# Two last blocks of a retention and MLP kernel: a third first-layer group as seven products, the second layer started inside the first, and own banks for its third product

## The chip, the cores and the metric

One core of a Trainium2 chip runs the whole program. The metric is the device time of one execution in microseconds (us): the median of three runs of the kernel before is 298.36 us (298.1 to 300.1).

## The reference

Eight batches of eight heads, 576 positions, head width 64, go through a causal retention (scores times a decay mask, no softmax). Its output, regrouped to 4608 tokens of 512 features, goes through a two-layer MLP with a tanh gelu between the layers:

```python
scores = scale * q @ k.T                       # per batch and head
ret = scores * Dmat                            # Dmat[i, j] = gamma_h ** (i - j) for i >= j, else 0
x = (ret @ v).transpose(0, 2, 1, 3).reshape(4608, 512)
h = x @ w_in                                   # 512 -> 2048
g = 0.5 * h * (1 + tanh(c * (h + 0.044715 * h**3)))
out = g @ w_out                                # 2048 -> 512
```

## The kernel before

The tokens are worked off in nine blocks of 512 (`NTB` = 9; the code calls a block `t`). Blocks 0 to 7 hold the first 512 positions of the eight batches; block 8 holds the last 64 positions of all of them, the tails. While the MLP of one block runs, the attention of the next batches is threaded in between: `at(t, u, f)` books a piece of work for step `u` of block `t`, and the loop at the end of the kernel runs it when that step has been issued. Nothing reorders the work after that: each engine executes its instructions in the order in which the code issues them, so the order in the loop is the order on TensorE (PE), VectorE (DVE), ScalarE (ACT) and on the store queues of SP and ACT.

**First layer.** `up(t, fc)` computes one group of 128 of the 2048 hidden features for all 512 tokens: four matmuls 128x512 into one PSUM bank `hp` (L471), then one gelu on ACT (L477) into `gT`. In blocks 7 and 8 (`WIN`) the first two double groups are instead done by `up_prod(t, j, m)`: the 2x2 block product over tokens x features is made by seven products instead of eight (a Strassen-Winograd scheme). One product is four matmuls 128x256 (L560). The seven products of group `j` go into three banks hA, hB and hC; between them ACT copies a bank to SBUF (L580, L586), DVE adds (L567) or copies (L588), and four gelus (L570) write `gT`. The operand sums of the weights (`in_sums`, L517) and of the tokens (`x_sums`, L536) are made on DVE beforehand, in the second layer of block 6 and of the block before. `W_ORDER` is the order by hand: "12" is product 2 of group 1, an empty token is one `up`, "a2" is `act_sums` for group 2.

**Second layer.** It is done by seven products too, in all blocks from 1 on. `act_sums` (L643 to L646) makes four sums of `gT` per group of two features on DVE, the third of them in place. `prod(t, m, u)` is product `m` for token half `u`: eight matmuls 128x256 (L661), with banks opA to opD. `after(t, m, u)` empties them: after product 1 an ACT copy (L691) keeps bank A, product 2 then goes on adding into the same bank, and a second ACT copy (L707) writes the lower half of output tile `o0`; DVE adds (L675) make the rest. In blocks 7 and 8 the order of products is 1, 4, 6, 5, 7, 2, 3, each for both halves. Products 5 and 3 share bank C: 3 adds on top of 5.

**Stores.** A block's two output tiles leave by `send`. For block 8 `send` calls `end` (L688), which writes 64 rows of one batch per DMA, one on SP's queue and one on ACT's: four DMAs of 128 KB for `o1` after product 7, four of 64 KB for the lower half of `o0` after product 2, and two plus two of 64 KB after the two halves of product 3.

PSUM has eight banks; `bank` takes the one longest free, `drop` gives it back at once in issue order, and the next user waits on the chip for the last reader.

Of the kernel before, what the change touches and what calls it, by code (L numbers as in the profile page):

```python
# [20 lines left out]
def kernel(  # L21
# [476 lines left out]
        )  # L498
        drop(hp)

    WIN = {t: 2 for t in (NTB - 2, NTB - 1)}
    GW = max(WIN.values())
    wi = {}

    def in_sums(j, ns):
        if not wi:
            for n in "234":
                wi[n] = sb.tile([128, 2, 256 * GW], F16, tag="ld", name="wi" + n, bufs=LD)
        c, lo, hi = slice(256 * j, 256 * j + 256), slice(256 * j, 256 * j + 256), slice(DF // 2 + 256 * j, DF // 2 + 256 * j + 256)
        b11, b12, b21, b22 = w_in_sb[:, 0:2, lo], w_in_sb[:, 0:2, hi], w_in_sb[:, 2:4, lo], w_in_sb[:, 2:4, hi]  # L510
        t2, t3, t4 = (wi[n][:, :, c] for n in "234")
        for n in ns:
            o, x, y, f = {
                3: (t3, b22, b12, ALU.subtract), 2: (t2, t3, b11, ALU.add),
                4: (t4, b21, t2, ALU.subtract), 1: (b12, b12, b11, ALU.subtract),
            }[n]
            nc.vector.tensor_tensor(out=o, in0=x, in1=y, op=f)  # L517
# [3 lines left out]
    def x_sums(t):  # L521
        if not xw:
            for n in ("12", "34"):
                x = sb.tile([128, 2, 4, 2, TL], F16, tag="ld", name="x" + n, bufs=LD)
                xw[int(n[0])], xw[int(n[1])] = x[:, 0], x[:, 1]
            for n in range(2):
                for s in "svu":
                    wk[s, n] = sb.tile([128, 512], F32, tag="ld", name="w" + s, bufs=LD)
        o = 8 * (t % 2) if t < B else GM
        x = xT[:, o : o + 8]  # L530
        a11, a12, a21, a22 = x[:, 0:4, 0:2], x[:, 0:4, 2:4], x[:, 4:8, 0:2], x[:, 4:8, 2:4]
        for s, x, y, f in (
            (xw[1], a21, a22, ALU.add), (xw[2], xw[1], a11, ALU.subtract),
            (xw[3], a11, a21, ALU.subtract), (xw[4], a12, xw[2], ALU.subtract),
        ):
            nc.vector.tensor_tensor(out=s, in0=x, in1=y, op=f)  # L536

    wk, wb = {}, {}

    def up_prod(t, j, m):  # L540
        if t not in gT:
            gT[t] = sb.tile([128, NF, NI, 128], F16, tag="gT", name="gT", bufs=1)
        o = 8 * (t % 2) if t < B else GM
        lo, hi = 256 * j, DF // 2 + 256 * j
        xh = lambda u, k: lambda kt: xT[:, o + 4 * u : o + 4 * u + 4, 2 * k + kt, :]
        xs = lambda n: lambda kt: xw[n][:, :, kt, :]
        ws = lambda k, c: lambda kt, i: w_in_sb[:, 2 * k + kt, c + 128 * i : c + 128 * i + 128]
        wt_ = lambda n: lambda kt, i: wi[n][:, kt, lo + 128 * i : lo + 128 * i + 128]
        tag, x, w = {
            1: ("B", xh(0, 0), ws(0, lo)), 2: ("A", xh(0, 1), ws(1, lo)), 3: ("C", xs(4), ws(1, hi)),  # L550
            4: ("B", xh(1, 1), wt_("4")), 5: ("C", xs(1), ws(0, hi)), 6: ("B", xs(2), wt_("2")),
            7: ("B", xs(3), wt_("3")),
        }[m]
        new = m in (1, 2, 5)
        if new:
            wb[j, tag] = bank("h" + tag)
        pb = wb[j, tag]
        for i in range(2):
            for kt in range(2):
                nc.tensor.matmul(  # L560
                    pb[:, 256 * i : 256 * i + 256].rearrange("p (g t) -> p g t", t=TL), w(kt, i), x(kt),
                    start=(new and i == kt == 0), stop=(kt == 1), skip_group_check=True,
                )
        s, v, u3 = (wk[n, j % 2] for n in "svu")

        def add(o, a, b):
            nc.vector.tensor_tensor(out=o, in0=a, in1=b, op=ALU.add)  # L567

        def gelu(x, u, f):
            nc.scalar.activation(  # L570
                out=gT[t][:, f : f + 2, 2 * u : 2 * u + 2, :].rearrange("p f i n -> p f (i n)"),
                in_=x.rearrange("p (f n) -> p f n", f=2), func=AF.Gelu_apprx_tanh,
            )

        def free(tag):
            drop(wb.pop((j, tag)))

        f = 2 * j
        if m == 1:
            nc.scalar.copy(out=s, in_=pb)  # L580
        elif m == 2:
            add(s, s, pb)
            free("A")
            gelu(s, 0, f)
        elif m == 6:
            nc.scalar.copy(out=v, in_=pb)  # L586
        elif m == 7:
            nc.vector.tensor_copy(out=u3, in_=pb)  # L588
            add(u3, u3, wb[j, "C"])
            gelu(u3, 1, NH + f)  # L590
        elif m == 4:
            gelu(pb, 1, f)
            free("B")
        elif m == 3:
            add(v, v, pb)
            free("C")
            gelu(v, 0, NH + f)
# [35 lines left out]

    gs = {}

    def act_sums(t, f0, f1, us=slice(0, 2)):
        if t not in gs:
            gs[t] = {n: sb.tile([128, NH, 2, 128], F16, tag="s" + n, name="s" + n, bufs=1) for n in ("1", "2", "4")}
        g = gT[t].rearrange("p f (u i) n -> p f u i n", i=2)
        lo, hi = slice(f0, f1), slice(NH + f0, NH + f1)  # L640
        a11, a12, a21, a22 = g[:, lo, us, 0], g[:, hi, us, 0], g[:, lo, us, 1], g[:, hi, us, 1]
        s = {n: x[:, lo, us] for n, x in gs[t].items()}
        nc.vector.tensor_tensor(out=s["1"], in0=a21, in1=a22, op=ALU.add)  # L643
        nc.vector.tensor_tensor(out=s["2"], in0=s["1"], in1=a11, op=ALU.subtract)
        nc.vector.tensor_tensor(out=a21, in0=a11, in1=a21, op=ALU.subtract)
        nc.vector.tensor_tensor(out=s["4"], in0=a12, in1=s["2"], op=ALU.subtract)  # L646

    def prod(t, m, u):
        g = gT[t].rearrange("p f (u i) n -> p f u i n", i=2)
# [4 lines left out]
        }[m]  # L654
        rhs = {1: W11, 2: W21, 3: W22, 4: wt["4"], 5: wt["1"], 6: wt["2"], 7: wt["3"]}[m]
        tag = {1: "A", 2: "A", 3: "C", 4: "D" if t in WIN else "B", 5: "C", 6: "B", 7: "B"}[m]
        new = m in (1, 6, 5) or tag == "D"
        if new and u == 0:
            op[tag] = bank("op" + tag)
        for f in range(NH):  # L660
            nc.tensor.matmul(  # L661
                op[tag][:, HD * u : HD * u + HD], lhs(f), rhs[:, f],
                start=(new and u == 0 and f == 0), stop=(f == NH - 1), skip_group_check=True,
            )

    keep = {}

    def after(t, m, u):
        last = t == NTB - 1
        if u == 0 and not (last and m == 3) or m == 4 and t in WIN:  # L670
            return
        def pr(tag):
            return op[tag].rearrange("p (u d) -> p u d", u=2)
# [18 lines left out]
        elif m == 6:  # L692
            keep["u2"] = sb.tile([128, 2, HD], F32, tag="k2", name="k2", bufs=1)
            add(keep["u2"], keep["s1"], pr("B"))
        elif m == 7:
            keep["u3"] = sb.tile([128, 2, HD], F32, tag="k3", name="k3", bufs=1)
            add(keep["u3"], keep["s1"], pr("B"))
            keep["o1"] = ost()
            add(keep["o1"][:, :, HD:DM], keep["u3"], pr("C"))
            if t in WIN:  # L700
                drop(op.pop("B"))
                add(keep["o1"][:, :, 0:HD], keep["u3"], pr("D"))
                drop(op.pop("D"))
                send(keep["o1"], 1)
        elif m == 2:
            keep["o0"] = ost()
            nc.scalar.copy(out=keep["o0"][:, :, 0:HD], in_=pr("A"))  # L707
            drop(op.pop("A"))
            if last:
                for v in range(2):  # L710
                    end(keep["o0"][:, v], 0, v, slice(0, HD))
        elif m == 3 and last:
            add(keep["o0"][:, u, HD:DM], keep["u2"][:, u], pr("C")[:, u])
            end(keep["o0"][:, u], 0, u, slice(HD, DM))
        elif m == 3:
            add(keep["o0"][:, :, HD:DM], keep["u2"], pr("C"))
            drop(op.pop("C"))
            send(keep["o0"], 0)
        elif m == 4:
            add(keep["o1"][:, :, 0:HD], keep["s1"], pr("B"))  # L720
            drop(op.pop("B"))
# [89 lines left out]
        for f in events.pop((t, u, last), ()):  # L811
            f()

    W_ORDER = "01 02 p 05 06 p 11 07 p 12 15 04 p 16 03 p 17 a2 p p 14 13 a0 p a1 a3".replace("p", "").split(" ")
    for n in range(2):
        at(NTB - 3, 17 + 2 * n, lambda n=n: in_sums(n, (3, 2)))
        at(NTB - 3, 21 + 2 * n, lambda n=n: in_sums(n, (4, 1)))
    at(NTB - 3, 27, lambda: x_sums(NTB - 2))
    at(NTB - 2, 17, lambda: x_sums(NTB - 1))

# [132 lines left out]
    for t in range(NTB):  # L953
# [7 lines left out]
        else:  # L961
# [7 lines left out]
            todo = deque(f + h for f in range(2 * WIN.get(t, 0), NH) for h in (0, NH))  # L969
            for w in (W_ORDER if t in WIN else ()):  # L970
                def mixed(w=w):
                    if not w:
                        up(t, todo.popleft())
                    elif w[0] == "a":
                        act_sums(t, 2 * int(w[1]), 2 * int(w[1]) + 2)
                    else:
                        up_prod(t, int(w[0]), int(w[1]))
                steps.append((mixed, 0 if w[:1] == "a" else 1 if w else 2))
            for f in range(0 if t == 1 or t in WIN else NH):
                steps.append(lambda f=f: up(t, f))  # L980
                def hi(f=f):
# [1 line left out]
                    if f % 2:  # L983
                        return lambda: act_sums(t, f - 1, f + 1)
                steps.append(hi)
            for m in (1, 4, 6, 5, 7, 2, 3) if t in WIN else (1, 6, 5, 7, 2, 4, 3):
                for u in range(2):
                    steps.append(lambda m=m, u=u: (prod(t, m, u), after(t, m, u)))
        size = sum(s[1] for s in steps if type(s) is tuple)
        u = done = 0  # L990
        for s in steps:
# [41 lines left out]
```

## Time and profile before

| what | us |
|---|---|
| median of three runs | 298.36 (298.1 to 300.1) |
| the profiled execution | 297.95 |
| its span, first to last instruction | 296.1 |
| PE, DVE, ACT, POOL busy | 283.0, 183.5, 165.9, 99.9 |
| block 7: first layer | 238.50 to 252.53 |
| block 7: second layer | 252.53 to 264.87 |
| block 8: first layer | 264.87 to 278.00 |
| block 8: second layer, last matmul's row ends | 278.00 to 290.89 |
| end of the span after that | 5.2 |

The stages are read from the chain of waits, which gives start and length of each piece of the chain that ended last. A row of the timeline gives the start, the time from the first start to the last end of a run of equal instructions, the engine, the line, the tiles and the count. A matmul's row has its drain at the end: 16 matmuls 128x256 are listed with 1.91 us, and the next ones start 1.75 us after them.

### The profile page before, as it was taken

Reading aid. Unit: us, or ns where it says so; the run is one execution under the profiler, and the core shown is the slowest. Engines: PE = TensorE matmul, PEld = TensorE weight load, DVE = VectorE, ACT = ScalarE, POOL = GpSimd, SP = SyncE. Lnnn points to the kernel's source line nnn. Section 1 sums busy time; section 2 is a strip of 40 time slices with the busy share of each in tenths; the row PEclk is TensorE's granted clock in tenths of the full one; section 3 lists DMA queues with packets and bytes.
Section 4 is the critical chain, followed back from the end, with each engine's and each line's share of the span. In section 5 each row is a group of like instructions: output and inputs, shape, how many; then the busy total and the mean of one; then the engine's idle time right before and its main releaser. Section 6 shows DMA issues by size and latency. Waiting matters only on the chain.

```text
span 296.1 us, 7458 instructions
## 1 busy us (share of the span) xinstructions
PE 283.0 (96%) x3076; PEld 202.0 (68%) x3076; DVE 183.5 (62%) x382; ACT 165.9 (56%) x309; POOL 99.9 (34%) x133
## 2 busy tenths in 40 slices
PE   6779999999999999999999999999999999999992
PEld 2458745888874588458845884488548876886781
DVE  6791506789754874477448744765487867934851
ACT  5377443998239653865386737663765357317600
POOL 4687486960880092008600730067030000000000
PEclk9999999999999999999999999999999999999998
DMA  6999999999969998999799869935931030011005
GB/s 198 310 366 366 341 321 292 273 283 214 201 153 225 214 229 181 253 206 192 95 290 218 148 123 263 216 75 102 254 74 38 2 142 0 2 72 73 0 2 142
DMA packets 129057, 52.91 MB, mean 179 GB/s; under 512 B 101632, under 2 KB 120576, under 8 KB 129024
## 3 DMA queue, kind: packets, MB, share of 16 engines
q1 hardware_dynamic: 128544, 51.92, 75.2%
q10 hardware_dynamic: 480, 0.52, 0.6%
q8 instruction: 24, 0.39, 0.6%
q14 instruction: 9, 0.07, 0.1%
HBM read 36.70 MB, written 9.44 MB: 156 GB/s over the span
## 4 chain that ended last, share of the span: by engine, by line
PE 92%; DVE 3%; ACT 1%; DMA 1%; issue 1%; POOL 0%; SPq 0%; POOLq 0%; DVEq 0%
PE hp L471 28%; PE opB L661 13%; PE opC L661 10%; PE opA L661 10%; PE hp L489 9%; PE op L607 4%; PE hB L560 2%; PE xs L450 2%; PE st L374 2%; PE tr L287 2%; PE xs L441 2%; PE opD L661 1%; PE hC L560 1%; PE xs L364 1%; DMA ld<-in_q_dram 1%; PE st L323 1%
## 5 line engine op out<-in xcount | busy, mean ns | idle before, releaser
L471 PE MATMUL hp<-xT,w_in_sb 128*128 128x512 f16 x384 | 86.9, 379 | 0.0
L477 ACT ACTIVATE gT<-hp 128x512 f16<-128x512 f32 x96 | 54.9, 595 | 31.0 <-PE hp L471 30.5
L471 PEld LDWEIGHTS <-w_in_sb 128*128 128x128 f16 x384 | 37.0, 98 | 40.7
L661 PEld LDWEIGHTS <-gT 128*128 128x128 f16 x512 | 49.0, 98 | 6.6 <-issue 0.2
L661 PEld LDWEIGHTS <-s 128*128 128x128 f16 x384 | 37.0, 98 | 5.6 <-issue 0.7
L643 DVE TENSOR_TENSOR s<-gT 128x512 f16<-128x512 f16 x32 | 14.3, 448 | 28.0 <-ACT gT L477 27.0
L941 POOL COPY gate<-s 128x1 f16<-128x1 f16 x5 | 0.9, 188 | 90.7 <-DVE s L646 90.7
L489 PE MATMUL hp<-xT,w_in_sb 128*128 128x256 f16 x256 | 30.2, 273 | 0.8 <-POOL w_in_sb L735 0.8
L661 PE MATMUL opA<-w_out_sb,gT 128*128 128x256 f16 x256 | 30.6, 273 | 0.0
L425 ACT CAST tbd<-ws 64x256 f16<-64x256 f32 x48 | 19.4, 403 | 16.4 <-DVE ws L416 15.8
L489 PEld LDWEIGHTS <-w_in_sb 128*128 128x128 f16 x256 | 24.5, 98 | 4.5 <-POOL w_in_sb L735 1.1
L661 PE MATMUL opB<-wt,gT 128*128 128x256 f16 x224 | 27.0, 273 | 0.0
L707 ACT COPY ost<-opA 128x512 f32<-128x512 f32 x8 | 4.7, 585 | 38.3 <-PE opA L661 21.7
L383 DVE TENSOR_TENSOR ret<-st,cm 128x512 f16<-128x512 f32 x40 | 24.8, 681 | 0.0
L675 DVE TENSOR_TENSOR k<-k,opB 128x512 f32<-128x512 f32 x16 | 11.0, 687 | 17.8 <-PE opB L661 10.4
L266 POOL TENSOR_TENSOR cq<-ld,sc 128x512 f16<-128x512 f32 x20 | 21.7, 1086 | 0.0
L266 POOL TENSOR_TENSOR ck<-ld,sc 128x512 f16<-128x512 f32 x20 | 21.0, 1049 | 0.0
L460 ACT CAST xT<-xs 128x512 f16<-128x512 f32 x36 | 19.3, 592 | 3.0 <-PE xs L364 1.5
L495 ACT ACTIVATE gT<-hp 128x512 f16<-128x512 f32 x32 | 18.5, 602 | 3.4 <-PE hp L489 3.0
L293 ACT COPY tt<-tr 128x1024 f16<-128x1024 f16 (+1 forms) x12 | 11.8, 998 | 11.1 <-PE tr L287 11.1
L675 DVE TENSOR_TENSOR ost<-k,opC 128x512 f32<-128x512 f32 (+1 forms) x17 | 11.1, 656 | 8.8 <-PE opC L661 8.5
L416 DVE TENSOR_TENSOR ws<-vs,gt 128x256 f32<-128x256 f32 x24 | 15.8, 659 | 1.1
(119 smaller groups left out, 415.1 us busy)
## 6 DMA issues: line engine op xcount, KB each, us to landing
ld<-in_q_dram SPq DMA_DIRECT2D x32, 256.0 KB, 5.2
ld<-in_k_dram SPq DMA_DIRECT2D x32, 256.0 KB, 5.4
ld<-in_v_dram SPq DMA_DIRECT2D x32, 256.0 KB, 5.4
out_dram<-ost SPq DMA_DIRECT2D x16, 512.0 KB, 3.3
ld<-in_moe_w_in_dram SPq DMA_DIRECT2D x16, 256.0 KB, 5.7
ld<-in_moe_w_out_dram SPq DMA_DIRECT2D x16, 256.0 KB, 5.3
lt<-in_k_dram SPq DMA_DIRECT2D x8, 128.0 KB, 5.3
lt<-in_q_dram SPq DMA_DIRECT2D x8, 128.0 KB, 4.6
```

The costliest lines, as they stand in the source:

```text
L266: eng.tensor_tensor(out=dst.rearrange("p (h d) -> p h d", d=D), in0=raw.rearrange("p (h d) -> p h d", d=D), in1=sc[:, s0].unsqueeze(2).to_ ...
L383: nc.vector.tensor_tensor(out=r.rearrange("p (n i) -> p n i", i=128), in0=t.rearrange("p (n i) -> p n i", i=128), in1=(cm if b < PAIR else ...
L416: nc.vector.tensor_tensor(out=w, in0=uc, in1=gt, op=ALU.mult)
L425: cp(out=(tbd[b % 2][r, c, :, r] if c < NC - 1 else tbt[b % NT4][r, :, r]), in_=w[r])
L460: nc.scalar.copy(out=xT[:, g0 : g0 + 2], in_=xs.rearrange("p (n g t) -> p g n t", n=HP, g=2))
L471: nc.tensor.matmul(hp.rearrange("p (g t) -> p g t", t=TL), w_in_sb[:, ct, 128 * fc : 128 * fc + 128], xT[:, o : o + TB // TL, ct, :], star ...
L477: nc.scalar.activation(out=gT[t][:, fc].rearrange("p i n -> p (i n)"), in_=hp, func=AF.Gelu_apprx_tanh)
L489: nc.tensor.matmul(hp[:, 256 * x : 256 * x + 256].rearrange("p (g t) -> p g t", t=TL), w_in_sb[:, ct, 128 * (f + x) : 128 * (f + x) + 128] ...
L495: nc.scalar.activation(out=gT[t][:, f : f + 2, 2 * u : 2 * u + 2, :].rearrange("p f i n -> p f (i n)"), in_=hp.rearrange("p (f n) -> p f n ...
L643: nc.vector.tensor_tensor(out=s["1"], in0=a21, in1=a22, op=ALU.add)
L661: nc.tensor.matmul(op[tag][:, HD * u : HD * u + HD], lhs(f), rhs[:, f], start=(new and u == 0 and f == 0), stop=(f == NH - 1), skip_group_ ...
L675: nc.vector.tensor_tensor(out=o, in0=a, in1=b, op=ALU.add)
```

## The change

1. `WIN` goes from 2 to 3: in blocks 7 and 8 a third group of four feature groups (group 2) is done by seven products, and four `up` are left of eight. The weight sums of three groups take six tiles instead of three, and are booked at steps 17 to 22 of block 6 instead of 17, 19, 21 and 23.
2. `W_ORDER` is new. Product 1 of the second layer ("Q0" and "Q1", its two token halves) stands inside the first layer's order. `act_sums` is split: parts 0 (three sums) stand in `W_ORDER`, the fourth sum is made after product 6.
3. A gelu of `up_prod` is put off by one token: `due` holds it until the next token's instructions have been issued.
4. The second layer's order in blocks 7 and 8 is 1, 4 (half 1), 2, 6, 5, 7, 4 (half 0), 3. Product 3 has a bank of its own, in block 8 one for each half (E and F); product 5 is added to `u2` on DVE instead, by an add that is new. The four stores of `o0`'s lower half in block 8 are now issued after product 2, ahead of `o1`'s.

The few words that came with the change also name "one batch a store"; `end`, which writes one batch per store, is the same before and after.

```diff
-    WIN = {t: 2 for t in (NTB - 2, NTB - 1)}
+    WIN = {t: 3 for t in (NTB - 2, NTB - 1)}
@@ in_sums
-            for n in "234":
-                wi[n] = sb.tile([128, 2, 256 * GW], F16, tag="ld", name="wi" + n, bufs=LD)
+            for g in range(0, GW, 2):
+                for n in "234":
+                    wi[n, g // 2] = sb.tile([128, 2, 512], F16, tag="ld", name="wi" + n, bufs=LD)
@@ x_sums
-            for n in range(2):
-                for s in "svu":
+            for n in range(3):
+                for s in "svu" if n < 2 else "vu":
@@ up_prod
-        s, v, u3 = (wk[n, j % 2] for n in "svu")
+        s, v, u3 = wk["s", j % 2], wk["v", j % 3], wk["u", j % 3]
         def gelu(x, u, f):
-            nc.scalar.activation(
-                out=gT[t][:, f : f + 2, 2 * u : 2 * u + 2, :].rearrange("p f i n -> p f (i n)"),
-                in_=x.rearrange("p (f n) -> p f n", f=2), func=AF.Gelu_apprx_tanh,
-            )
+            g = gT[t][:, f : f + 2, 2 * u : 2 * u + 2, :].rearrange("p f i n -> p f (i n)")
+            due.append(lambda: nc.scalar.activation(
+                out=g, in_=x.rearrange("p (f n) -> p f n", f=2), func=AF.Gelu_apprx_tanh
+            ))
         elif m == 4:
             gelu(pb, 1, f)
-            free("B")
+            due.append(lambda: free("B"))
@@ prod
+        if t in WIN and m == 3:
+            tag = "EF"[u if t == NTB - 1 else 0]
-        new = m in (1, 6, 5) or tag == "D"
+        new = tag not in op
@@ after
         elif m == 6:
             add(keep["u2"], keep["s1"], pr("B"))
+            for f in range(0, NH if t in WIN else 0, 2):
+                act_sums(t, f, f + 2, parts=(1,))
         elif m == 7:
             add(keep["u3"], keep["s1"], pr("B"))
             keep["o1"] = ost()
             add(keep["o1"][:, :, HD:DM], keep["u3"], pr("C"))
-            if t in WIN:
-                drop(op.pop("B"))
-                add(keep["o1"][:, :, 0:HD], keep["u3"], pr("D"))
-                drop(op.pop("D"))
-                send(keep["o1"], 1)
+            drop(op.pop("B")) if t in WIN else None
+            drop(op.pop("C")) if t in WIN else None
+        elif m == 5 and t in WIN:
+            add(keep["u2"], keep["u2"], pr("C"))
         elif m == 3 and last:
-            add(keep["o0"][:, u, HD:DM], keep["u2"][:, u], pr("C")[:, u])
+            add(keep["o0"][:, u, HD:DM], keep["u2"][:, u], pr("EF"[u])[:, u])
             end(keep["o0"][:, u], 0, u, slice(HD, DM))
+        elif m == 4 and t in WIN:
+            add(keep["o1"][:, :, 0:HD], keep["u3"], pr("D"))
+            drop(op.pop("D"))
+            send(keep["o1"], 1)
@@ the order
-    W_ORDER = "01 02 p 05 06 p 11 07 p 12 15 04 p 16 03 p 17 a2 p p 14 13 a0 p a1 a3".replace("p", "").split(" ")
-    for n in range(2):
+    W_ORDER = (
+        "01 02 05 11 06 12 p 15 07 16 21 22 p 04 25 17 03 26 14 p 13 27 p Q0 24 a0 23 a1 Q1 a3 a2"
+    ).replace("p", "").split(" ")
+    for n in range(GW):
         at(NTB - 3, 17 + 2 * n, lambda n=n: in_sums(n, (3, 2)))
-        at(NTB - 3, 21 + 2 * n, lambda n=n: in_sums(n, (4, 1)))
+        at(NTB - 3, 18 + 2 * n, lambda n=n: in_sums(n, (4, 1)))
@@ the loop over blocks
                 def mixed(w=w):
+                    put_off = list(due)
+                    due.clear()
+                    token(w)
+                    for f in put_off:
+                        f()
+                def token(w):
                     if not w:
                         up(t, todo.popleft())
-                    elif w[0] == "a":
-                        act_sums(t, 2 * int(w[1]), 2 * int(w[1]) + 2)
+                    elif w[0] == "Q":
+                        prod(t, 1, int(w[1]))
+                        after(t, 1, int(w[1]))
+                    elif w[0] in "ab":
+                        act_sums(t, 2 * int(w[1]), 2 * int(w[1]) + 2, parts=("ab".index(w[0]),))
-            for m in (1, 4, 6, 5, 7, 2, 3) if t in WIN else (1, 6, 5, 7, 2, 4, 3):
-                for u in range(2):
-                    steps.append(lambda m=m, u=u: (prod(t, m, u), after(t, m, u)))
+            two = [(m, u) for m in (1, 6, 5, 7, 2, 4, 3) for u in range(2)]
+            if t in WIN:
+                two = [(4, 1), (2, 0), (2, 1), (6, 0), (6, 1), (5, 0), (5, 1), (7, 0), (7, 1), (4, 0), (3, 0), (3, 1)]
+            for m, u in two:
+                steps.append(lambda m=m, u=u: (prod(t, m, u), after(t, m, u)))
```

More of the change, by code (lines that the diff above doesn't have):

```diff
@@ L506, in in_sums @@
         if not wi:
-            for n in "234":
-                wi[n] = sb.tile([128, 2, 256 * GW], F16, tag="ld", name="wi" + n, bufs=LD)
-        c, lo, hi = slice(256 * j, 256 * j + 256), slice(256 * j, 256 * j + 256), slice(DF // 2 + 256 * j, DF // 2 + 256 * j + 256)
+            for g in range(0, GW, 2):
+                for n in "234":
+                    wi[n, g // 2] = sb.tile([128, 2, 512], F16, tag="ld", name="wi" + n, bufs=LD)
+        c, lo, hi = slice(256 * (j % 2), 256 * (j % 2) + 256), slice(256 * j, 256 * j + 256), slice(DF // 2 + 256 * j, DF // 2 + 256 * j + 256)
         b11, b12, b21, b22 = w_in_sb[:, 0:2, lo], w_in_sb[:, 0:2, hi], w_in_sb[:, 2:4, lo], w_in_sb[:, 2:4, hi]
-        t2, t3, t4 = (wi[n][:, :, c] for n in "234")
+        t2, t3, t4 = (wi[n, j // 2][:, :, c] for n in "234")
         for n in ns:
@@ L536, in x_sums @@
             nc.vector.tensor_tensor(out=s, in0=x, in1=y, op=f)
-    wk, wb = {}, {}
+    wk, wb, due = {}, {}, []
     def up_prod(t, j, m):
@@ L543, in up_prod @@
         o = 8 * (t % 2) if t < B else GM
-        lo, hi = 256 * j, DF // 2 + 256 * j
+        lo, hi, c = 256 * j, DF // 2 + 256 * j, 256 * (j % 2)
         xh = lambda u, k: lambda kt: xT[:, o + 4 * u : o + 4 * u + 4, 2 * k + kt, :]
@@ L547, in up_prod @@
         ws = lambda k, c: lambda kt, i: w_in_sb[:, 2 * k + kt, c + 128 * i : c + 128 * i + 128]
-        wt_ = lambda n: lambda kt, i: wi[n][:, kt, lo + 128 * i : lo + 128 * i + 128]
+        wt_ = lambda n: lambda kt, i: wi[n, j // 2][:, kt, c + 128 * i : c + 128 * i + 128]
         tag, x, w = {
@@ L634, with act_sums @@
     gs = {}
-    def act_sums(t, f0, f1, us=slice(0, 2)):
+    def act_sums(t, f0, f1, us=slice(0, 2), parts=(0, 1)):
         if t not in gs:
@@ L642, in act_sums @@
         s = {n: x[:, lo, us] for n, x in gs[t].items()}
[L643 to L646, printed above, removed]
+        if 0 in parts:
+            nc.vector.tensor_tensor(out=s["1"], in0=a21, in1=a22, op=ALU.add)
+            nc.vector.tensor_tensor(out=s["2"], in0=s["1"], in1=a11, op=ALU.subtract)
+            nc.vector.tensor_tensor(out=a21, in0=a11, in1=a21, op=ALU.subtract)
+        if 1 in parts:
+            nc.vector.tensor_tensor(out=s["4"], in0=a12, in1=s["2"], op=ALU.subtract)
     def prod(t, m, u):
@@ L656, in prod @@
         tag = {1: "A", 2: "A", 3: "C", 4: "D" if t in WIN else "B", 5: "C", 6: "B", 7: "B"}[m]
-        new = m in (1, 6, 5) or tag == "D"
-        if new and u == 0:
+        if t in WIN and m == 3:
+            tag = "EF"[u if t == NTB - 1 else 0]
+        new = tag not in op
+        if new:
             op[tag] = bank("op" + tag)
@@ L662, in prod @@
                 op[tag][:, HD * u : HD * u + HD], lhs(f), rhs[:, f],
-                start=(new and u == 0 and f == 0), stop=(f == NH - 1), skip_group_check=True,
+                start=(new and f == 0), stop=(f == NH - 1), skip_group_check=True,
             )
@@ L669, in after @@
         last = t == NTB - 1
-        if u == 0 and not (last and m == 3) or m == 4 and t in WIN:
+        if u == 0 and not (last and m == 3 or t in WIN and m == 4) or u == 1 and t in WIN and m == 4:
             return
@@ L708, in after @@
             drop(op.pop("A"))
-            if last:
-                for v in range(2):
-                    end(keep["o0"][:, v], 0, v, slice(0, HD))
+            for v in range(2 if last else 0):
+                end(keep["o0"][:, v], 0, v, slice(0, HD))
+        elif m == 5 and t in WIN:
+            add(keep["u2"], keep["u2"], pr("C"))
         elif m == 3 and last:
-            add(keep["o0"][:, u, HD:DM], keep["u2"][:, u], pr("C")[:, u])
+            add(keep["o0"][:, u, HD:DM], keep["u2"][:, u], pr("EF"[u])[:, u])
             end(keep["o0"][:, u], 0, u, slice(HD, DM))
         elif m == 3:
-            add(keep["o0"][:, :, HD:DM], keep["u2"], pr("C"))
-            drop(op.pop("C"))
+            x = "E" if t in WIN else "C"
+            add(keep["o0"][:, :, HD:DM], keep["u2"], pr(x))
+            drop(op.pop(x))
             send(keep["o0"], 0)
+        elif m == 4 and t in WIN:
+            add(keep["o1"][:, :, 0:HD], keep["u3"], pr("D"))
+            drop(op.pop("D"))
+            send(keep["o1"], 1)
         elif m == 4:
@@ L971, in mixed @@
                 def mixed(w=w):
+                    put_off = list(due)
[4 more added lines that the diff above has]
+                def token(w):
                     if not w:
                         up(t, todo.popleft())
-                    elif w[0] == "a":
-                        act_sums(t, 2 * int(w[1]), 2 * int(w[1]) + 2)
+                    elif w[0] == "Q":
[3 more added lines that the diff above has]
+                        act_sums(t, 2 * int(w[1]), 2 * int(w[1]) + 2, parts=("ab".index(w[0]),))
                     else:
                         up_prod(t, int(w[0]), int(w[1]))
-                steps.append((mixed, 0 if w[:1] == "a" else 1 if w else 2))
+                steps.append((mixed, 0 if w[:1] in ("a", "b", "Q") else 1 if w else 2))
             for f in range(0 if t == 1 or t in WIN else NH):
```

## The prediction

> **What bounds the kernel now.** The page comes first: busy shares, then the chain of waits by engine. TensorE (PE) holds 92% of the chain that ended last, so time is gained where PE has less to do or waits less, or after its last matmul.
>
> ```profile
> PE 283.0 (96%) x3076; PEld 202.0 (68%) x3076; DVE 183.5 (62%) x382; ACT 165.9 (56%) x309; POOL 99.9 (34%) x133
> PE 92%; DVE 3%; ACT 1%; DMA 1%; issue 1%; POOL 0%; SPq 0%; POOLq 0%; DVEq 0%
> ```
>
> The change touches only the end, so next come the busy times of its four stages: first and second layer of block 7, then of block 8. PE is busy throughout until the last stage; in the first layers ACT and DVE have three to five us to spare each.
>
> ```profile
> 238.30:252.40 14.10, 14.10 (x114) 9.32 (x112) 9.43 (x18) 10.21 (x20) 0.00 (x0) 1.00 0.19 74
> 252.40:264.70 12.30, 12.30 (x118) 10.97 (x113) 8.11 (x20) 2.57 (x5) 0.00 (x0) 1.00 0.03 12
> 264.70:277.80 13.10, 13.10 (x90) 8.61 (x88) 7.13 (x13) 9.06 (x18) 0.00 (x0) 1.00 0.19 72
> 277.80:291.40 13.60, 12.58 (x113) 10.84 (x111) 8.12 (x19) 2.64 (x5) 0.00 (x0) 1.00 0.10 30
> ```
>
> Then the chain of waits in order of time, for the price of one product (four 128x256) and one `up` (four 128x512):
>
> ```profile
> 276.70 0.44 PE hC L560 x4
> 277.14 0.86 PE hp L471 x4
> 278.00 1.75 PE opA L661 x16
> ```
>
> Last, the timeline of the end, in order of start: the two halves of product 3 (L661), the adds (L675), the copy of bank A (L707), and the stores on the two queues (SPq, ACTq).
>
> ```profile
> 286.77 0.69 DVE L675 TENSOR_TENSOR k<-k,opB 128x512 f32<-128x512 f32 x1 [2.74 <-PE opB L661]
> 288.10 0.68 DVE L675 TENSOR_TENSOR ost<-k,opD 128x512 f32<-128x512 f32 x1
> 288.31 1.04 PE L661 MATMUL opC<-w_out_sb,s 128*128 128x256 f16 x8
> 288.81 1.46 ACTq L688 DMA_DIRECT2D out_dram<-ost  x2
> 289.39 0.42 DVE L675 TENSOR_TENSOR ost<-k,opC 128x256 f32<-128x256 f32 x1 [0.61 <-PE opC L661]
> 289.86 1.03 PE L661 MATMUL opC<-w_out_sb,s 128*128 128x256 f16 x8 [0.51 <-DVE ost L675]
> 290.39 0.58 ACT L707 COPY ost<-opA 128x512 f32<-128x512 f32 x1 [9.97 <-DVE ost L675]
> 290.93 0.42 DVE L675 TENSOR_TENSOR ost<-k,opC 128x256 f32<-128x256 f32 x1 [1.12 <-PE opC L661]
> 291.00 2.71 ACTq L688 DMA_DIRECT2D out_dram<-ost  x4
> ```
>
> Two things to see. The second half of product 3 starts 1.55 after the first, though eight matmuls need 8 x 0.109 = 0.87: it waits 0.68 for the add that reads the shared bank. And the copy of bank A, ready since product 2 ended, starts at 290.39 only, because ACT is busy issuing two stores until 290.27; the stores of `o0` queue up behind it, and the last is issued at 293.71, 2.39 before the span ends at 296.1.
>
> **The change, part by part** (in us; minus is gained).
>
> *A third group by seven products.* Per block PE loses four `up` (4 x 0.863, from 8.63 for ten) and gets seven products (7 x 0.437, from 1.75 for four): -3.45 + 3.06 = -0.39. Two blocks: **-0.78**. Unless the rows change, only the waits below can move this.
>
> By the Trainium skill (TensorE: Matmul & The Clock Gate, Back-to-back issue gap), a stream of weight loads and matmuls sustains about 131 ns at N=512 and 81 ns at N=128, so whole groups would be cheap; with an estimate of 98 ns at 256 between these, seven products would cost 2.74 against 2.10, and the step would lose 1.3 in two blocks instead of gaining 0.78. The trace has 216 ns and 109 ns here, and its rows decide.
>
> *ACT and DVE for it.* Per block ACT gets two copies and four gelus for four gelus, DVE two copies-or-adds and two adds more (4 x 0.69 = 2.8) and an add after product 5 (0.69). In the first layer they fit the spare time above. The added add and the four fourth sums moved behind product 6 lie beside products 5 and 7 (3.5 of PE), where DVE waits 2.74 before its next add now; product 3 needs them only after that. Cost 0, and at most 0.7 per block if that cover were gone.
>
> *Waits inside the first layer.* With three groups in flight, a bank is refilled two to three products after its last use. I laid the new order out on the three engines with the rows' durations: a gelu or copy lets the next ACT operation start after 0.49 to 0.54 (two gelus are listed with 1.07 together), DVE's 0.69 after 0.61, a handoff costs 0.03 to 0.09. Late are: product 3 of group 2 in block 7 (0.04, for DVE), products 4 of group 1 and 7 of group 2 in block 8 (0.08 and 0.13). Sum **+0.25**, from 0 to 1.2 if each of some 20 handoffs were 0.05 later. The old order's own losses in block 8 (0.91 for two products, 0.51 for one) go: **-0.1**.
>
> *Product 1 inside, product 2 early.* Product 2 adds into bank A, so PE waits for ACT's copy of it (L691). It had 7 us of cover; now it has the half of product 4. The chain, from the last matmul of "23": DVE add 0.69, ACT gelu 0.54, copy 0.58, and 0.3 of drain and handoffs, 2.1 in all. PE's cover is the second half of product 1 and one half of product 4, 2 x 0.87. So 0.37 in block 8 (0.11 of it already in product 1, whose fifth weight load waits for the gelu of "24"). In block 7 the tails' matmuls (0.5) lie between as well, but DVE is behind by three sums and ACT by the tails' cast: 0.26. Sum **+0.63**; 0.3 if the chain runs 0.15 faster in each block, 1.2 if one more 0.58 copy stands ahead once. The queue behind that copy on ACT is empty. Product 6 needs the second sum of group 2 only by its fifth matmul, some 0.3 after I find it ready.
>
> *Weight sums in block 6.* Four more DVE sums, and two pulled ahead: the add that frees bank B (k, L675) has six sums ahead instead of two, so it starts 2.24 / 1.57 later: 232.56 + 1.57 = 234.13, and ends at 234.81. PE writes that bank at 234.83 now: **+0.03**, up to 0.4 if DVE runs as late as its rows allow. The token sums wait for product 4 in both kernels.
>
> *Own banks for product 3.* The 0.68 wait goes; the adds are the same. **-0.68**. The first half's add is late next (behind the add of `o1`), but it now holds up only its store.
>
> *The stores at the end.* The four low-half stores and the copy go 8 us forward. SP and ACT issue them beside PE, with nothing queued behind. From the end of product 7, DVE needs 2.05 for its three adds (286.73 to 288.78, the same adds as now); the half of product 4 and both of 3 take 3 x 0.87 = 2.62, so `o1`'s stores start 0.54 before PE's end. ACT issues them for 1.46, then the last two for 1.24 (the last two rows of ACTq, 292.48 to 293.71): the last issue ends 2.2 after PE's end, and 2.39 later the span ends: 4.6, against 296.1 - 290.9 = 5.2. **-0.6**; nothing if issues and landings do not pull together, -1.5 if the stores follow the last add at once.
>
> The Trainium skill (DMA: Bandwidth & Descriptors, Issuing engines are not separate DMA queues) says that starting a DMA takes a time that is usually small beside the DMA itself; taken so, the order of issue would give nothing, and the sum would be 0.6 higher. Here the issues of one queue fill 2.7 of the 5.2, by the rows above.
>
> Sum: -0.78 + 0.25 - 0.1 + 0.63 + 0.03 - 0.68 - 0.6 = **-1.25**. The profiled execution took 297.95 (span 296.1): 296.7 after. The median of the three runs is 0.41 above it, 298.36: I predict **297.1**.
>
> **Rivals.**
>
> *No new wait shows* (chance 0.10). For it: PE lost little to waits in the old mixed stages. Against: the copy's chain is 2.1 long and its cover 1.75. Without the 0.91 of new waits: 296.2.
>
> *The end is no shorter* (0.10). For it: landings take 2.0 to 2.9 by the list of DMA issues, and `o1`'s four stores of 128 KB now run beside the last. Against: two fewer issues per queue behind PE. Without the 0.6: 297.7.
>
> *ACT paces the first layers, slower than before* (0.10). From the first copy to the copy of bank A ACT has 23 operations in block 8 and 25 in block 7, at a mean step of 0.51 (11.7 and 12.7), beside 12.9 and 13.7 of PE (12.62 of first layer and 0.87 of product 1 less the 0.6 before the first copy; block 7 with 0.8 for the tails). If each step took its whole row (0.59 to 0.63), it would be 13.9 and 15.1: 2.4 more than PE has in both, of which the 0.63 is part, so +1.8 and 298.9. It turns the sign from a mean step of about 0.59. Against it speak the rows with two gelus in 1.07.
>
> *The change doesn't do what it says*: that the stores become one batch each is so already; it moves their order only. Nothing is priced for it.
>
> **How the numbers follow.** The forecast has 0.70, the rivals 0.10 each. All bounds at their best give 298.36 - 2.8 = 295.5, at their worst +1.4, 299.8. The range leaves out a tenth at each end: 296.0 to 298.9, which takes in all three rivals. 1% is 3.0, about what a measurement of this kernel can tell from no change. Faster by more would need all gains at their upper bound and no new wait: 0.02. Slower by more would need ACT's rival twice over: 0.04. Within: 0.94.
>
> **What would show it.** Block 8's first layer with Q0 and Q1 shorter by some 0.2 net; a wait of 0.2 to 0.4 of opA for ACT's copy in both blocks; no wait between the halves of product 3; 4.6 from PE's last row to the span's end. Wrong would be: waits of hA, hB or hC over 1 us in sum; ACT without gaps from 241 to 254; a wait for DVE at the head of product 6; or a last store issued over 2.5 after PE's end.

## The result, and the profile after

The changed kernel takes 297.04 us (median of 22 runs, 296.27 to 298.53) against 298.10 us for the kernel before (22 runs): a ratio of 0.9958, interval 0.9942 to 0.9975, a gain of 1.06 us. Predicted were 297.1 us and a gain of 1.25 us. The profiled executions differ by 1.56 us (297.95 and 296.39), their spans by 1.4 us; the profiled execution of the changed kernel lies 0.65 below its median, that of the kernel before 0.15.

The page of the changed kernel, busy times: PE has less to do, DVE 8 us more, ACT 2.5 us more, and little of that is on the path to the end (the waits in block 8 below).

```profile
PE 282.2 (96%) x3100; PEld 204.3 (69%) x3100; DVE 191.7 (65%) x396; ACT 168.4 (57%) x313; POOL 100.2 (34%) x133
```

The same four stages of the changed kernel (start and end, length, busy time and count of PE, weight loads, DVE, ACT and POOL, then the granted clock, the DMA engines' busy share and GB/s):

```profile
238.38:252.85 14.47, 14.47 (x134) 11.20 (x131) 10.92 (x20) 11.74 (x22) 0.00 (x0) 1.00 0.19 73
252.85:264.35 11.50, 11.50 (x113) 10.23 (x108) 9.80 (x23) 2.18 (x4) 0.00 (x0) 1.00 0.00 1
264.35:278.40 14.05, 14.05 (x114) 10.84 (x111) 9.37 (x16) 11.16 (x21) 0.00 (x0) 1.00 0.20 76
278.40:289.90 11.50, 11.37 (x103) 9.71 (x100) 8.74 (x20) 1.75 (x4) 0.00 (x0) 1.00 0.10 24
```

The first layers now hold product 1 as well, so the pairs count: block 7 is 25.97 us instead of 26.37, and PE is busy to the hundredth. (The drain, by which a row of four matmuls outlasts the start of the next by 0.16, covers shorter waits in these sums; they are read from the starts.) In block 8's last stage PE's idle time has shrunk from 0.52 (13.60 less 12.58, less the 0.50 by which that window reaches beyond PE's end) to 0.13 (11.50 less 11.37).

The timeline of the end, with the same kinds of row as in the prediction:

```profile
287.30 0.69 DVE L680 TENSOR_TENSOR k<-k,opB 128x512 f32<-128x512 f32 x1 [0.80 <-PE opB L666]
287.97 1.04 PE L666 MATMUL opE<-w_out_sb,s 128*128 128x256 f16 x8
288.62 0.68 DVE L680 TENSOR_TENSOR ost<-k,opD 128x512 f32<-128x512 f32 x1
288.84 1.04 PE L666 MATMUL opF<-w_out_sb,s 128*128 128x256 f16 x8
289.22 0.41 DVE L680 TENSOR_TENSOR ost<-k,opE 128x256 f32<-128x256 f32 x1
289.33 2.39 SPq L693 DMA_DIRECT2D out_dram<-ost  x4
289.34 2.67 ACTq L693 DMA_DIRECT2D out_dram<-ost  x4
289.92 0.42 DVE L680 TENSOR_TENSOR ost<-k,opF 128x256 f32<-128x256 f32 x1 [0.28 <-PE opF L666]
```

The halves of product 3 start 0.87 apart: no wait. But look at the last two rows together. The last add is done at 290.34, and the two stores that need it are the last of four in each queue: ACT issues until 292.01. The stores, not PE, are what the end waits for. The chain of waits of this profile does not show it: it ends with this add and leads back through PE.

Block 7 starts between 237.9 and 240.3 us in the profiles of this study, though nothing ahead of the last sums of block 6 differs. So I compare the stretch from block 7's first product to the end of the span, cut by rows: block 7; block 8 up to the end of PE's last row; and what follows, split at the end of the last store's issue.

| kernel | block 7 | block 8 | to last issue's end | from there | stretch |
|---|---|---|---|---|---|
| before | 26.37 | 26.19 | 2.82 | 2.40 | 57.78 |
| changed | 25.97 | 25.53 | 2.13 | 2.67 | 56.31 |
| changed, second profile | 25.97 | 25.53 | 2.13 | 2.93 | 56.56 |

The last row is the changed kernel profiled a second time: PE's stages and the queue repeat to 0.01, what follows the last issue varies by 0.26.

### The profile page after: what moved, and what is told of

Same layout as the page of the kernel before. It is cut to its first block, busy times and chain, and to the rows that moved or that the text cites. A ratio compares the mean times of both kernels' runs of the same rounds, so it can differ in the third digit from the quotient of the medians.

```text
span 294.7 us, 7531 instructions
## 1 busy us (share of the span) xinstructions
PE 282.2 (96%) x3100; PEld 204.3 (69%) x3100; DVE 191.7 (65%) x396; ACT 168.4 (57%) x313; POOL 100.2 (34%) x133
## 5 line engine op out<-in xcount | busy, mean ns | idle before, releaser
L471 PE MATMUL hp<-xT,w_in_sb 128*128 128x512 f16 x352 | 79.0, 379 | 0.0
L477 ACT ACTIVATE gT<-hp 128x512 f16<-128x512 f32 x88 | 50.6, 597 | 31.0 <-PE hp L471 30.4
L471 PEld LDWEIGHTS <-w_in_sb 128*128 128x128 f16 x352 | 34.0, 98 | 38.2
L489 PEld LDWEIGHTS <-w_in_sb 128*128 128x128 f16 x256 | 24.5, 98 | 4.9 <-POOL w_in_sb L745 1.6
L495 ACT ACTIVATE gT<-hp 128x512 f16<-128x512 f32 x32 | 18.5, 602 | 3.8 <-PE hp L489 3.5
L666 PE MATMUL opC<-wt,s 128*128 128x256 f16 x128 | 15.5, 273 | 0.0
```

Of the source, the lines that this page charges most:

```text
L471: nc.tensor.matmul(hp.rearrange("p (g t) -> p g t", t=TL), w_in_sb[:, ct, 128 * fc : 128 * fc + 128], xT[:, o : o + TB // TL, ct, :], star ...
L477: nc.scalar.activation(out=gT[t][:, fc].rearrange("p i n -> p (i n)"), in_=hp, func=AF.Gelu_apprx_tanh)
L489: nc.tensor.matmul(hp[:, 256 * x : 256 * x + 256].rearrange("p (g t) -> p g t", t=TL), w_in_sb[:, ct, 128 * (f + x) : 128 * (f + x) + 128] ...
L495: nc.scalar.activation(out=gT[t][:, f : f + 2, 2 * u : 2 * u + 2, :].rearrange("p f i n -> p f (i n)"), in_=hp.rearrange("p (f n) -> p f n ...
L666: nc.tensor.matmul(op[tag][:, HD * u : HD * u + HD], lhs(f), rhs[:, f], start=(new and f == 0), stop=(f == NH - 1), skip_group_check=True,)
```

## Experiments

**Own banks undone.** `tag = "EF"[u if t == NTB - 1 else 0]` becomes

```diff
+            tag = "E"
```

> The changed kernel with one thing undone: in block 8 the two halves of product 3 share one bank again. If the own banks are worth what the prediction put down (the wait between the halves lies on the path to the end), the second half waits about 0.9 us for the add that reads the bank, and the span grows by 0.9. Rival: the last store waits for ACT's queue anyway (in the changed kernel its issue starts at 291.46, 1.1 after the last add is done), so the wait shows on PE, about 0.9, and the span does not move (within 0.15).

Measured: block 8 26.37, stretch 56.34 (changed: 25.53 and 56.31); 296.61 us, ratio 0.992 (0.9887 to 0.9952). Timeline of the end:

```profile
289.43 2.68 ACTq L693 DMA_DIRECT2D out_dram<-ost  x4
289.79 1.03 PE L666 MATMUL opE<-w_out_sb,s 128*128 128x256 f16 x8 [0.68 <-DVE ost L680]
290.86 0.42 DVE L680 TENSOR_TENSOR ost<-k,opE 128x256 f32<-128x256 f32 x1 [1.12 <-PE opE L666]
```

PE loses 0.84, the last add ends as much later from block 7's start, and ACT's queue is the same row as in the changed kernel, 2.68 long from the same add of `o1`. Counted from block 7's first product, the last issue ends at 53.64 (changed: 53.63). The rival holds.

**Own banks alone, in the kernel before.**

```diff
+        if t == NTB - 1 and m == 3:
+            tag = "EF"[u]
-        new = m in (1, 6, 5) or tag == "D"
+        new = tag not in op
...
+        if last and m == 2:
+            nc.vector.tensor_tensor(
+                out=keep["u2"], in0=keep["u2"], in1=op["C"].rearrange("p (u d) -> p u d", u=2), op=ALU.add
+            )
```

> The kernel before with one part of the change alone: in block 8 the halves of product 3 have a bank each, and product 5 is added on DVE after product 2. By the prediction's term for the own banks, PE's 0.68 us of waiting goes and the span falls by 0.68. Rival, since the run with one bank in the changed kernel cost PE 0.84 and the span nothing: PE ends 0.7 earlier, but the last stores stand in ACT's queue behind the lower half of the same tile, and the span stays within 0.15.

Measured: block 8 25.53 (0.66 less than before), stretch 57.83 (0.05 more); 298.25 us, ratio 0.9992 (0.9965 to 1.0019). PE ends at 290.74, and ACT still issues `o1`'s stores first, then copies, then issues four:

```profile
289.32 1.46 ACTq L694 DMA_DIRECT2D out_dram<-ost  x2
290.90 0.59 ACT L713 COPY ost<-opA 128x512 f32<-128x512 f32 x1 [9.97 <-PE opF L663]
291.52 2.69 ACTq L694 DMA_DIRECT2D out_dram<-ost  x4
```

Again the rival holds, from the other side: the last issue ends 55.36 after block 7's first product, against 55.37 before.

**The second layer alone.** `WIN` back to 2, the old `W_ORDER`, gelus issued with their token, and

```diff
-                two = [(4, 1), (2, 0), (2, 1), (6, 0), (6, 1), (5, 0), (5, 1), (7, 0), (7, 1), (4, 0), (3, 0), (3, 1)]
+                two = [(1, 0), (1, 1), (4, 1), (2, 0), (2, 1), (6, 0), (6, 1), (5, 0), (5, 1), (7, 0), (7, 1), (4, 0), (3, 0), (3, 1)]
```

> The changed kernel with its first layer as before: two groups by seven products, the old order of the first layer, gelus not put off, product 1 after the first layer. Left of the change are the second layer's new order, the own banks and the order of the stores. If these make most of the gain, PE has no new wait over 0.1 us, the stretch from block 7's first product to the end of the span falls by 1.0 to 1.3 against the kernel before, and the third group with the join is worth 0.1 to 0.4 on top. Rival, by the prediction's terms: it falls by 0.6 (0.68 and 0.6 less the wait for bank A), and the first layer makes the rest.

Measured: block 7 26.38, block 8 25.50, last issue 2.14 after PE, stretch 56.94; 296.81 us, ratio 0.994 (0.9914 to 0.9965). That is 0.84 less than before, between the two theories; 0.5 more came after the last issue (2.91 against 2.40), without which it would be 1.35. PE shows no wait over 0.1. So the third group, the join and the gelus put off are together worth 0.41 in block 7 and nothing in block 8 (25.53 against 25.50). Against the run with own banks alone PE's block 8 is the same (25.50 and 25.53), but the last issue ends 2.14 after PE instead of 3.47: that 1.33 comes from the new order of products and stores, which no run parts.

**The join undone.**

```diff
-        "... p 13 27 p Q0 24 a0 23 a1 Q1 a3 a2"
+        "... p 13 27 p 24 a0 23 a1 a3 a2 Q0 Q1"
```

> The changed kernel with the join undone: product 1 of the second layer (both halves) stands after the last token of the first layer instead of inside it. If the join pays, products of group 2 that stood behind Q0 now wait for bank readers on DVE and for their gelus, about 0.3 to 0.45 us a block, and the span grows by 0.7. Rival: the join only moves the wait (0.28 us for ACT's copy of bank A in block 8 goes away, since 2.6 us of products cover it now): the span stays, within 0.2, or falls by up to 0.3.

Measured: block 7 26.62, block 8 25.63, stretch 57.27, 0.96 more (0.75 in PE's stages); 297.42 us, ratio 0.9951 (0.9918 to 0.9984). The chain of waits of block 7:

```profile
249.50 0.45 PE hB L561 x4
249.95 0.03 DVEq L589
249.98 0.36 DVE wv L568
250.34 0.61 DVE wu L589
250.96 0.02 issue
250.98 0.70 DVE wu L568
251.68 0.04 issue
251.72 0.60 PE hC L561 x4
```

The chain leaves PE for three DVE operations, 249.98 to 251.68. Meanwhile PE has too little to do: it waits 0.20 ahead of product 4 of group 2 (251.00) and 0.28 ahead of product 3 (251.72, which is 0.72 after product 4 began instead of its 0.44). Product 1 inside the order is what fills that place. The wait for ACT's copy is gone, as the rival said, but it was the smaller. Both blocks are also longer here than with two groups and no join (26.38 and 25.50, the run with the second layer alone): the third group paid only together with the join.

**Two groups, joined.** `WIN` back to 2, with this order:

```diff
+        "01 02 p 05 06 p 11 07 p 12 15 04 p 16 03 p 17 p p Q0 14 a2 13 a0 p Q1 a1 a3"
```

> The changed kernel with two groups as seven products instead of three, and product 1 still inside the first layer. By the price of the products alone (-0.39 us a block for the third group) the span grows by 0.8. Rival: the waits that three groups in flight bring (0.2 us inside block 8's first layer and 0.3 for the copy of bank A) go as well, and the span grows by only 0.2 to 0.4.

Measured: block 7 26.89, block 8 25.91, stretch 57.83; 297.66 us, ratio 0.9964 (0.9931 to 0.9997). PE's stages are 1.3 longer, more than either theory. The order I wrote has a wait of its own: product 1 starts straight after the `up` whose gelu it needs (its eighth matmul waits 0.33 in block 7 and 0.23 in block 8 for that gelu). It tells nothing of the third group's worth; the run with the second layer alone does.

**Two batches in a store.**

```diff
-            for h, e in enumerate((nc.sync, nc.scalar)):
-                r0 = S * (b + h) + M0
-                e.dma_start(out=out[r0 : r0 + TL, d], in_=o[TL * h : TL * h + TL, d])
+            e = (nc.sync, nc.scalar)[v]
+            e.dma_start(
+                out=out[S * b : S * b + 2 * S, :].rearrange("(h s) d -> h s d", h=2)[:, M0:S, d], in_=o[:, d]
+            )
```

> The changed kernel with two batches in one store in block 8 (128 rows of SBUF, half as many stores; token half 0 on SP's queue and half 1 on ACT's). If the issues on the queues set the end, the last issue starts about 0.9 us earlier and the span shrinks by 0.8 to 1.1. Rival: the landing sets it (a store of twice the size lands later by as much), and the span stays within 0.3.

Measured: 310.94 us, ratio 1.0394 (1.0328 to 1.046); stretch 70.80. The issues shrank as hoped, the last ending 1.01 after PE. Then SP waits, by its view of waits, for one landing:

```profile
SPq L1053 <- DMA out_dram<-ost: 17.6, 1, 17.6
```

ACT's queue moved 480 packets in six stores in the changed kernel, and 390 in three here, for the same 384 rows:

```profile
q10 hardware_dynamic: 480, 0.52, 0.6%
q10 hardware_dynamic: 390, 0.52, 0.5%
```

480 is 384 + 6 x 16, and 390 is 384 + 3 x 2. The Trainium skill (DMA: Bandwidth & Descriptors, Why a DMA increments its semaphore by 16 and not by 1) says that a copy runs on the largest number of engines up to 16 that divides the slowest dimension of both sides, each ending with one write to the semaphore. That agrees with both counts: the outer dimension of the destination is 2 here, 64 in the other. Neither the 0.8 to 1.1 less nor the rival's 0.3 came.

**Two of `o1`'s stores from POOL.**

```diff
-            for h, e in enumerate((nc.sync, nc.scalar)):
+            for h, e in enumerate((nc.sync, nc.scalar) if i == 0 or v == 0 else (nc.gpsimd, nc.gpsimd)):
```

> The changed kernel with two of the four stores of o1 in block 8 issued by POOL, which is idle there, so that SP and ACT have one store less each ahead of the last ones. If the two queues set the end, the last issue starts 0.6 to 0.7 us earlier and the span shrinks by 0.5 to 0.7. Rival: a store issued by POOL lands later than the last ones do now, and the span stays or grows by up to 1.

Measured: the last issue ends 1.49 after PE instead of 2.13, but the span 5.16 after PE instead of 4.81: stretch 56.66; 296.94 us, ratio 0.9947 (0.9927 to 0.9968). The list of DMA issues (KB each, median us from issue to landing):

```profile
out_dram<-ost POOLq DMA_DIRECT2D x2, 128.0 KB, 3.2
out_dram<-ost SPq DMA_DIRECT2D x1, 128.0 KB, 2.4
out_dram<-ost ACTq DMA_DIRECT2D x4, 64.0 KB, 2.8
```

The span stayed or grew a little (0.35 against the changed kernel's first profile, 0.10 against its second), as the rival said, but not for its reason. POOL issues its second store until 290.92, and both of its stores land by 293.6 (3.2 after they start). The last one of ACT starts at 290.87 and lands 3.3 later, at 294.1, where it took 2.3 in the changed kernel. So a shorter queue alone brought nothing here, since the last landings came later; why they did was not settled. Whether the issues or the landings limit the way from `o1`'s adds to the end is therefore open.

**Product 7 before 5.** Order 4, 2, 6, 7, 5, 3, bank G for product 7, and

```diff
         elif m == 5 and t in WIN:
+            add(keep["o1"][:, :, HD:DM], keep["u3"], pr("C"))
+            send(keep["o1"], 1)
             add(keep["u2"], keep["u2"], pr("C"))
```

> The changed kernel with the second layer's order 4 (both halves), 2, 6, 7, 5, 3, product 7 in a bank of its own, and the stores of o1 sent after product 5. Both halves of product 4 now cover ACT's copy of bank A, and the stores of o1 start about 1.0 us before PE's end instead of 0.55. If the copy of bank A and the queue of stores are what the changed kernel still waits for, PE's last row ends 0.3 us earlier and the span shrinks by 0.6 to 1.0. Rival: the landing of the last stores sets the end, and only PE's 0.3 is gained.

Measured: block 8 25.25, last issue 1.71 after PE, stretch 55.61: 0.70 less than the changed kernel in two parts as expected, 0.28 on PE and 0.42 in the queue. 296.74 us, ratio 0.9951 (0.9911 to 0.999); the times cannot tell that from the changed kernel, the stages can.

**One store for both token halves** (64 rows x 2 halves), in the changed kernel, in the kernel with 7 before 5, and with the shared bank:

```diff
+        def both(o, i, d=slice(0, DM)):
+            x = out.rearrange("(v b s) d -> b s v d", v=2, b=4)
+            for h, e in enumerate((nc.sync, nc.scalar)):
+                e.dma_start(out=x[2 * i + h, M0:S, :, d], in_=o[TL * h : TL * h + TL, :, d])
```

> The changed kernel with the stores of both token halves joined (64 rows x 2 halves a store) and nothing else. If issue time on the two queues sets the end, the stretch from block 7's first product to the end falls from 56.3 to 55.5 to 55.8. Rival: landing sets it, and it stays at 56.2 to 56.4; if a store with two pieces a row runs on fewer DMA engines, as the store of two batches did, it grows by more than 5.

> The kernel with product 7 before 5 and, on top, one store per queue for both token halves of a batch pair (64 rows x 2 halves) in block 8 where two stores stood: o1 and the lower half of o0 go out by two stores each instead of four. From block 7's first product to the end of the span it took 55.6 us with 7 before 5 alone, against 56.3 in the changed kernel and 57.8 in the kernel before. If the queue of stores is still last there, ACT's queue gets shorter by one issue (0.65 to 0.85) and the stretch falls to 55.0 to 55.2. Rival: a store over two halves lands later, or the last add sets the issue by then, and the stretch stays at 55.4 to 55.6.

> The kernel with joined stores for both token halves, and the two halves of product 3 in one bank again. In the changed kernel the shared bank cost PE 0.84 us and the span nothing, and I put that down to the queue of stores. If that is so, the shared bank must cost something as soon as the queue is shorter: 0.4 to 0.6 more than the run with joined stores alone. Rival: PE's last 0.84 is hidden by something other than the queue, and the two runs take the same, within 0.15.

> The changed kernel itself, unchanged, on the same chip as the others of this call, as their base: 56.3 us from block 7's first product to the end, a ratio of 0.996 to the kernel before.

| kernel | to last issue's end | from there | stretch | median us, ratio (interval) |
|---|---|---|---|---|
| changed again | 2.13 | 2.93 | 56.56 | 296.76, 0.9975 (0.9951 to 0.9999) |
| joined stores | 2.79 | 2.82 | 57.11 | 297.42, 0.9981 (0.997 to 0.9991) |
| joined, shared bank | 1.89 | 2.84 | 57.08 | 297.51, 0.9984 (0.9975 to 0.9994) |
| joined, 7 before 5 | 2.21 | 3.05 | 56.49 | 296.52, 0.9956 (0.9944 to 0.9967) |

Neither expectation nor rival of the two runs with own banks came: fewer stores, later end. The rows of ACT's queue with joined stores:

```profile
289.12 0.65 ACTq L691 DMA_DIRECT2D out_dram<-ost  x1
289.81 2.64 ACTq L696 DMA_DIRECT2D out_dram<-ost  x2
```

The 256 KB store is issued in 0.65, but the two small ones behind it take 2.64 where they took 1.2. So the queue is busy for longer with the same bytes in fewer stores, and the shared bank (0.84 later on PE) is hidden here too. That is the rival's number, but the test lacked its condition, a shorter queue, and so decides nothing between the two. The number of issues alone does not set the queue's time: ACT issued two stores in 1.55 with two batches in each, three in 3.34 here, and four in 2.67 in the changed kernel. What makes the later ones slow was not settled.

## Why the prediction was right, point by point

- **The third group** (-0.78): right as a count of matmuls. Block 7 lost 0.40 with no wait showing, 0.39 a block by the rows. That it needs the join to pay was not foreseen: the prediction books the join as a cost only (+0.63), and without it block 7 is 0.65 longer.
- **Waits inside the first layer** (+0.25): 0.19. Block 8 has exactly the two that were laid out, 0.07 and 0.12, each a product that takes 0.51 or 0.56 to the next instead of 0.44:

```profile
272.62 0.60 PE L561 MATMUL hB<-x,wi 128*128 128x256 f16 x4
273.13 0.60 PE L561 MATMUL hB<-xT,wi 128*128 128x256 f16 x4
274.43 0.60 PE L561 MATMUL hC<-x,w_in_sb 128*128 128x256 f16 x4
274.99 0.60 PE L561 MATMUL hB<-x,wi 128*128 128x256 f16 x4
```

- **Product 2 early** (+0.63): 0.33. In block 8 the chain is as predicted, and takes 0.28 between the half of product 4 and product 2 (1.15 apart instead of 0.87) and 0.05 in product 1:

```profile
278.03 1.09 PE L666 MATMUL opA<-w_out_sb,gT 128*128 128x256 f16 x8
278.23 0.69 DVE L568 TENSOR_TENSOR wv<-wv,hC 128x512 f32<-128x512 f32 x1
278.96 0.63 ACT L572 ACTIVATE gT<-wv 128x512 f16<-128x512 f32 x1 [0.50 <-DVE wv L568]
278.96 1.04 PE L666 MATMUL opD<-wt,gT 128*128 128x256 f16 x8
279.49 0.57 ACT L696 COPY k<-opA 128x512 f32<-128x512 f32 x1
```

  In block 7 the 0.26 did not show: the tails' matmuls cover 0.67 (252.31 to 252.98), not the 0.5 that I gave them. That is 0.17 of it; the rest is a chain a little shorter than laid out. The copy ends at 254.69, just ahead of product 2 at 254.74. The run with both halves of product 4 ahead of product 2 took the 0.28 away and nothing else on PE.
- **Weight sums** (+0.03): PE starts product 4 of block 6 at 234.89 instead of 234.83.
- **Own banks** (-0.68): this step failed as a cause. The wait went from PE as predicted, but two runs show that it was never on the path: undone, it costs the stretch 0.03, and alone it brings nothing (+0.05), with the last issue's end unmoved to 0.01 in both.
- **The stores** (-0.6): counted from PE's end, 4.81 instead of 5.22, so -0.41. The last issue ends 2.13 after PE (predicted 2.2); what follows took 2.67 instead of 2.39. To the last issue's end alone it is -0.69 (2.13 instead of 2.82); with the second profile, 0.26 longer behind it, -0.15 would be left of the -0.41.

The last two terms hold together and not apart. What counts is the way from product 7's adds through the queues; I had cut it at PE's end, so a wait of PE that moves this cut was booked as gain and the stores with the rest. Sum of both: -1.09 measured, -1.28 predicted. The old losses of PE in block 8 (-0.1) went. With -0.78 + 0.19 - 0.1 + 0.33 + 0.05 - 1.09 the sum is -1.40, the spans' difference.

That the time came out to 0.06 is partly luck. The gains at the end were forecast 0.19 too large and the wait for bank A 0.30 too large, and these two largely cancel. The forecast also started from a median of three runs, 298.36, where 22 runs gave 298.10; from there it would have been 296.85. One sum of the prediction is wrong as well: its worst bounds add up to about +1.2, and to +2.6 with the 0.7 per block that it allows for DVE, not to +1.4.

Of the rivals, new waits did show, 0.57 of the 0.91 that were priced; the end was shorter, by two thirds of the term, though what follows the last issue did grow, as that rival's landings would have it; ACT did not pace the first layers, which is plain from PE busy all of 14.47 in block 7 and all of 14.05 in block 8.

## What to carry to other kernels

At the end of a kernel, follow the last store back through its queue before pricing a wait on TensorE: here 0.84 us of PE cost nothing, since the same queue was still issuing earlier stores. The new second layer, with four stores 8 us forward, made most of the gain (1.36 of 1.75 up to the end of the last issue); that the stores are what did it, and not the order of products, is argued from the queues' rows, not shown. A third group by fewer products paid in full only where the engines' chain behind its last product was covered (block 7), and nothing net where it was not (block 8); without product 1 of the second layer inside the first it lost time in both. Lay a new order out on all engines with the rows' durations: the places and sizes of the waits in block 8 came out to 0.05.

## What the runs showed of the hardware that was not expected

- A store whose destination has an outer dimension of 2 had SP wait 17.6 us for its landing, with 2 instead of 16 closing packets a store.
- The same bytes in fewer stores held ACT's queue for 3.34 us (289.12 to 292.46) instead of 2.67, most of it in the small stores behind the 256 KB one.
- Two 128 KB stores issued by POOL took 3.2 us to land, one each from SP and ACT, first in their queues, 2.4 and 2.7 in the same run. The last 64 KB store from ACT took 3.3 there, and 2.3 in the changed kernel.
- From the end of the last issue to the end of the span, 2.40 to 3.05 us pass (the POOL and two-batch runs aside), 0.26 apart in two profiles of one kernel. The two kernels with all of `o0`'s stores behind `o1`'s have 2.40 and about 2.5, the others 2.67 or more. A gain below 0.26 at the end of a kernel is seen in the rows, not in the time.
